# Cutting the first 4 MB load of a DMA-bound kernel into 16 and 112 partitions

## The chip, the cores and the metric

One core of a Trainium2 chip. Times are device microseconds (us) of that core. "Time" is the median of several executions; the profile is of one execution, and its span is about 1.4 us shorter than that execution's time (before: 119.5 against 120.87 us). A "row" is the 32 KB that a transfer moves into one SBUF partition; in the traces it is one packet on one of the 16 DMA engines (1536 packets of 32 KB, 96 to an engine). From the prediction on, "engine" without a name means a DMA engine, and its "ring" is what has been issued to it and is still to be moved.

## The reference

```python
# x, y: (1024, 16, 512) bf16; gamma: (512,) bf16
def reference(x, y, gamma):
    return x + gamma * y
```

x, y and the result are 16.78 MB each. The 16384 rows of 512 elements are laid over 128 SBUF partitions, 128 rows to a partition, and worked in four pieces of 32 rows: 32 KB per partition, 4 MB per transfer.

## The kernel before

```python
PIECES = [32, 32, 32, 32]
X_AT = [0, 32, 0, 32]            # two buffers for x
SP = [('x', 0), ('y', 0), ('x', 1), ('y', 1), ('y', 2), ('x', 2), ('y', 3), ('x', 3)]
ACT = [('g',), ('s', 0, 0, 2), ('s', 1, 1, 2), ('s', 2, 2, 2), ('s', 3, 3, 3)]
...
xv = xf.rearrange("(p n) d -> p n d", p=P)     # partition p: 128 rows, contiguous in HBM
...
elif kind == "x":                # loads are issued from SyncE, in the order of SP
    c = args[0]
    i = eng.dma_start(out=x_tile(c), in_=xv[:, piece(c), :]).then_inc(s_x[c], 16)
...
for c in range(n):               # VectorE
    yt = y_sb[:, piece(c), :]
    _take(s_y[c], 16, nc.vector)
    nc.vector.tensor_tensor(out=yt, in0=yt, in1=gamma_sb[...], op=MULT).then_inc(s_dve, 1)
    _take(s_x[c], 16, nc.vector)
    _take(s_dve, 1, nc.vector)
    nc.vector.tensor_tensor(out=yt, in0=x_tile(c), in1=yt, op=ADD).then_inc(s_add, 1)
```

The third x waits for the first add, the fourth for the second; the four stores are issued from ScalarE after the third and the fourth add. The first x, the first y and gamma are moved to the head of the program.

Of the kernel before, what the change touches and what calls it, by code (L numbers as in the profile page):

```python
# [3 lines left out]


PIECES = [32, 32, 32, 32]

X_AT = [0, 32, 0, 32]
X_AFTER = [-1, -1, 0, 1]


SP = [('x', 0), ('y', 0), ('x', 1), ('y', 1), ('y', 2), ('x', 2), ('y', 3), ('x', 3)]
ACT = [('g',), ('s', 0, 0, 2), ('s', 1, 1, 2), ('s', 2, 2, 2), ('s', 3, 3, 3)]

EARLY = [('x', 0), ('y', 0), ('g',)]
MULT, ADD = mybir.AluOpType.mult, mybir.AluOpType.add


def _take(sem, n, eng):


    return eng.wait_ge(sem, n).then_inc(sem, -n)  # L22


def kernel(
    tc: tile.TileContext,
    x: bass.AP,
    y: bass.AP,
    gamma: bass.AP,
    out: bass.AP,  # L30
):



    nc = tc.nc
    P = nc.NUM_PARTITIONS
    tc.close()
    tc.compile()  # L38

    xf = x.flatten_outer_dims()  # L40
    yf = y.flatten_outer_dims()
    of = out.flatten_outer_dims()
    N, D = xf.shape
    rows = N // P
    n = len(PIECES)
    assert sum(PIECES) == rows
    starts = [sum(PIECES[:c]) for c in range(n + 1)]
    dt = xf.dtype
    xv = xf.rearrange("(p n) d -> p n d", p=P)
    yv = yf.rearrange("(p n) d -> p n d", p=P)  # L50
    ov = of.rearrange("(p n) d -> p n d", p=P)

    gamma_row = nc.alloc_sbuf_tensor("gamma_row", [1, D], dt).ap()
    ones_row = nc.alloc_sbuf_tensor("ones_row", [1, P], dt).ap()
    gamma_sb = nc.alloc_sbuf_tensor("gamma_sb", [P, D], dt).ap()
    y_sb = nc.alloc_sbuf_tensor("y_sb", [P, rows, D], dt).ap()
    x_rows = max(a + r for a, r in zip(X_AT, PIECES))
    x_sb = nc.alloc_sbuf_tensor("x_sb", [P, x_rows, D], dt).ap()
    gamma_ps = nc.alloc_psum_tensor("gamma_ps", [P, D], mybir.dt.float32).ap()

    sem = nc.alloc_semaphore
    s_gamma, s_ones, s_ps, s_dve = sem("s_gamma"), sem("s_ones"), sem("s_ps"), sem("s_dve")
    s_x = [sem(f"s_x{c}") for c in range(n)]
    s_y = [sem(f"s_y{c}") for c in range(n)]
    s_add, s_end, s_out = sem("s_add"), sem("s_end"), sem("s_out")

    def piece(a, b=None):
        return slice(starts[a], starts[(a if b is None else b) + 1])

    def x_tile(c):  # L70
        return x_sb[:, X_AT[c] : X_AT[c] + PIECES[c], :]

    early, stores = [], 0

    def ring(eng, what, known=-1):

        nonlocal stores
        for w in what:
            kind, args = w[0], w[1:]
            need = X_AFTER[args[0]] if kind == "x" else args[2] if kind == "s" else -1  # L80
            if need > known:
                eng.wait_ge(s_add, need + 1)
                known = need
            if kind == "g":
                i = eng.dma_start(out=gamma_row, in_=gamma.unsqueeze(0)).then_inc(s_gamma, 16)
            elif kind == "x":
                c = args[0]
                i = eng.dma_start(out=x_tile(c), in_=xv[:, piece(c), :]).then_inc(s_x[c], 16)
            elif kind == "y":
                c = args[0]  # L90
                i = eng.dma_start(out=y_sb[:, piece(c), :], in_=yv[:, piece(c), :])
                i.then_inc(s_y[c], 16)
            else:
                r = piece(args[0], args[1])
                i = eng.dma_start(out=ov[:, r, :], in_=y_sb[:, r, :]).then_inc(s_out, 16)
                stores += 1
            if w in EARLY:
                early.append(i.ins)

    ring(nc.sync, SP)  # L100
    ring(nc.scalar, ACT)


    nc.vector.memset(ones_row, 1.0).then_inc(s_ones, 1)  # L104
    _take(s_ones, 1, nc.tensor)
    _take(s_gamma, 16, nc.tensor)
    nc.tensor.matmul(gamma_ps, ones_row, gamma_row, start=True, stop=True).then_inc(s_ps, 1)  # L107
    _take(s_ps, 1, nc.vector)
    nc.vector.tensor_copy(out=gamma_sb, in_=gamma_ps).then_inc(s_dve, 1)  # L109
    _take(s_dve, 1, nc.vector)  # L110

    for c in range(n):
        yt = y_sb[:, piece(c), :]
        _take(s_y[c], 16, nc.vector)
        nc.vector.tensor_tensor(  # L115
            out=yt, in0=yt, in1=gamma_sb[:, None, :].to_broadcast([P, PIECES[c], D]), op=MULT
        ).then_inc(s_dve, 1)
        _take(s_x[c], 16, nc.vector)
        _take(s_dve, 1, nc.vector)
        nc.vector.tensor_tensor(out=yt, in0=x_tile(c), in1=yt, op=ADD).then_inc(s_add, 1)  # L120


    nc.scalar.sem_inc(s_end, 1)
    _take(s_end, 1, nc.sync)
    _take(s_add, n, nc.sync)
    _take(s_out, 16 * stores, nc.sync)

    main = nc.main_func.blocks[0].instructions
    names = {i.name for i in early}
    for b in nc.main_func.blocks[1:]:  # L130
        for i in [i for i in b.instructions if i.name in names]:
            b.instructions.remove(i)
    for k, i in enumerate(early):
        main.insert(1 + k, i)


# [1 line left out]
_INS = ['x', 'y', 'gamma']  # L138
_OUTS = [((1024, 16, 512), 'bfloat16')]


# [23 lines left out]
```

## Time and profile before

| | before |
|---|---|
| time, median of 6 runs | 120.34 us (120.29 to 121.09) |
| span of the profiled run | 119.5 us |
| share of the 16 DMA engines | 98.9% |
| one 32 KB row on one DMA engine | 1.213 us |

The prediction below shows the lines that carry this. Three more are needed here, from the page (the busy share of the DMA engines and the GB/s, in 40 slices of the span), from the view of the x buffer (time from issue to landing), and from the view of a stretch (start:end and length, busy times of the engines, granted clock, DMA share, GB/s):

```profile
DMA  7989898998998989898989999898989898989995
GB/s 208 494 373 504 351 526 351 384 493 351 384 493 351 526 351 526 351 515 362 493 384 471 406 428 450 384 493 351 526 351 526 351 526 351 515 362 471 406 471 230
```

```profile
DMA to landing us min/median/max: 12.1/21.5/30.3
```

```profile
5.20:10.05 4.85, 0.21 (x1) 0.00 (x0) 0.69 (x1) 0.00 (x0) 1.00 1.00 432
```

Single slices swing between 350 and 526 GB/s because all engines start their 32 KB packets at nearly the same time (the first at 0.99 to 1.60 us) and a packet counts in the slice in which it starts. A stretch of exactly four rows (4 x 1.213 = 4.85 us) gives the true rate, 432 GB/s. The first x lands 12.1 us after its issue, the shortest of the four.

### The profile page before, as it was taken

The numbers are of one execution on the slowest core, as the hardware profiler recorded it, in microseconds if no ns is written. First come the engines' busy times: TensorE is split into PE (matmuls) and PEld (weight loads), VectorE is DVE, ScalarE is ACT, GpSimd is POOL, SyncE is SP. The second block draws the span as 40 slices with busy tenths as digits, with TensorE's granted clock in tenths as the row PEclk, the third lists the DMA queues.
The fourth block names the chain that finished last, engine by engine and source line by source line (L and its number), as shares of the span: only waits on it lengthen the run. The fifth ranks groups of instructions, "written<-read, shape, count | busy, mean of one in ns | idle before, by whom it ended". The sixth has DMA issues, their size and how long they took to land. (4 is left out here: it accounts for less than half of the span.)

```text
span 119.5 us, 84 instructions
## 1 busy us (share of the span) xinstructions
PE 0.6 (0%) x1; PEld 0.1 (0%) x1; DVE 70.2 (59%) x10; POOL 0.2 (0%) x4
## 2 busy tenths in 40 slices
PE   0100000000000000000000000000000000000000
PEld 0000000000000000000000000000000000000000
DVE  0100000699999289999999999999999600000000
POOL 0000000000000000000000000000000000000000
DMA  7989898998998989898989999898989898989995
GB/s 208 494 373 504 351 526 351 384 493 351 384 493 351 526 351 526 351 515 362 493 384 471 406 428 450 384 493 351 526 351 526 351 526 351 515 362 471 406 471 230
DMA packets 1730, 50.33 MB, mean 421 GB/s; under 512 B 193, under 2 KB 194, under 8 KB 194
## 3 DMA queue, kind: packets, MB, share of 16 engines
q1 hardware_dynamic: 1152, 33.55, 66.4%
q10 hardware_dynamic: 578, 16.78, 32.5%
HBM read 33.56 MB, written 16.78 MB: 421 GB/s over the span
## 5 line engine op out<-in xcount | busy, mean ns | idle before, releaser
L115 DVE TENSOR_TENSOR y_sb<-y_sb,gamma_sb 128x16384 bf16<-128x16384 bf16 x4 | 34.8, 8688 | 18.4 <-DVEq L22 18.4
L120 DVE TENSOR_TENSOR y_sb<-x_sb,y_sb 128x16384 bf16<-128x16384 bf16 x4 | 34.8, 8692 | 0.6
L109 DVE CAST gamma_sb<-gamma_ps 128x512 bf16<-128x512 f32 x1 | 0.7, 692 | 3.4 <-DVEq L22 3.4
L104 DVE MEMSET ones_row<- 1x128 bf16 x1 | 0.2, 165 | 2.0 <-PEq L38 2.0
L107 PE MATMUL gamma_ps<-gamma_row,ones_row 1*128 1x512 bf16 x1 | 0.6, 580 | 4.8 <-PEq L22 4.8
L107 PEld LDWEIGHTS gamma_ps<-gamma_row,ones_row 1*128 1x128 bf16 x1 | 0.1, 100 | 4.8 <-issue 4.8
L149 POOL MEMSET const-bfloat16-1.0<- 128x1 bf16 x1 | 0.1, 101 | 0.0
L149 POOL MEMSET const-uint8-127<- 128x1 uint8 x1 | 0.1, 101 | 0.0
L149 POOL MEMSET const-float32-0.0<- 128x1 f32 x1 | 0.1, 98 | 0.2 <-issue 0.2
L149 POOL MEMSET const-float32-1.0<- 128x1 f32 x1 | 0.1, 98 | 0.0
## 6 DMA issues: line engine op xcount, KB each, us to landing
x_sb<-in_x_dram SPq DMA_DIRECT2D x4, 4096.0 KB, 21.5
y_sb<-in_y_dram SPq DMA_DIRECT2D x4, 4096.0 KB, 35.4
out_dram<-y_sb ACTq DMA_DIRECT2D x4, 4096.0 KB, 23.8
gamma_row<-in_gamma_dram ACTq DMA_DIRECT2D x1, 1.0 KB
```

What stands on the lines that cost most here:

```text
L104: nc.vector.memset(ones_row, 1.0).then_inc(s_ones, 1)
L107: nc.tensor.matmul(gamma_ps, ones_row, gamma_row, start=True, stop=True).then_inc(s_ps, 1)
L109: nc.vector.tensor_copy(out=gamma_sb, in_=gamma_ps).then_inc(s_dve, 1)
L115: nc.vector.tensor_tensor(out=yt, in0=yt, in1=gamma_sb[:, None, :].to_broadcast([P, PIECES[c], D]), op=MULT).then_inc(s_dve, 1)
L120: nc.vector.tensor_tensor(out=yt, in0=x_tile(c), in1=yt, op=ADD).then_inc(s_add, 1)
L149: nc = _bacc.Bacc("TRN2", target_bir_lowering=False, num_devices=1)
```

## The change

The intent: the DMA engines stand idle for the first 0.99 us. If the head of the program asks for 16 partitions first, one row for each engine, the engines might get their first row sooner, while the other 112 partitions are still being issued. The core of the diff (the rest rewrites how the lists of transfers are kept, and moves nothing):

```diff
+FIRST = 16
...
             elif kind == "x":
-                c = args[0]
-                i = eng.dma_start(out=x_tile(c), in_=xv[:, piece(c), :]).then_inc(s_x[c], 16)
+                to = x_sb[:, w[3] : w[3] + w[2] - w[1], :]
+                r = slice(w[1], w[2])
+                if w == x_loads[0]:
+                    i = eng.dma_start(out=to[:FIRST], in_=xv[:FIRST, r, :])
+                    early.append(i.then_inc(s_load[w], 16).ins)
+                    i = eng.dma_start(out=to[FIRST:], in_=xv[FIRST:, r, :])
+                else:
+                    i = eng.dma_start(out=to, in_=xv[:, r, :])
+                i.then_inc(s_load[w], 16)
...
-        _take(s_x[c], 16, nc.vector)
+                _take(s_load[w], 32 if w == x_loads[0] else 16, nc.vector)
```

More of the change, by code (lines that the diff above doesn't have):

```diff
@@ L6 @@
 PIECES = [32, 32, 32, 32]
-X_AT = [0, 32, 0, 32]
-X_AFTER = [-1, -1, 0, 1]
-SP = [('x', 0), ('y', 0), ('x', 1), ('y', 1), ('y', 2), ('x', 2), ('y', 3), ('x', 3)]
-ACT = [('g',), ('s', 0, 0, 2), ('s', 1, 1, 2), ('s', 2, 2, 2), ('s', 3, 3, 3)]
-EARLY = [('x', 0), ('y', 0), ('g',)]
+SP = [('x', 0, 32, 0), ('y', 0, 32), ('x', 32, 64, 32), ('y', 32, 64), ('y', 64, 96), ('x', 64, 96, 0), ('y', 96, 128), ('x', 96, 128, 32)]
+ACT = [('g',), ('s', 0, 32, 2), ('s', 32, 64), ('s', 64, 96), ('s', 96, 128)]
+EARLY = (2, 1)
+DVE = [('m', 0), ('a', 0), ('m', 1), ('a', 1), ('m', 2), ('a', 2), ('m', 3), ('a', 3)]
+FIRST = 16
 MULT, ADD = mybir.AluOpType.mult, mybir.AluOpType.add
@@ L56 @@
     y_sb = nc.alloc_sbuf_tensor("y_sb", [P, rows, D], dt).ap()
-    x_rows = max(a + r for a, r in zip(X_AT, PIECES))
+    x_loads = [w for w in SP + ACT if w[0] == "x"]
+    y_loads = [w for w in SP + ACT if w[0] == "y"]
+    stores = [w for w in SP + ACT if w[0] == "s"]
+    for loads in (x_loads, y_loads, stores):
+        assert sum(w[2] - w[1] for w in loads) == rows
+    x_rows = max(w[3] + w[2] - w[1] for w in x_loads)
     x_sb = nc.alloc_sbuf_tensor("x_sb", [P, x_rows, D], dt).ap()
@@ L62, with meets, pieces_of, x_at @@
     s_gamma, s_ones, s_ps, s_dve = sem("s_gamma"), sem("s_ones"), sem("s_ps"), sem("s_dve")
-    s_x = [sem(f"s_x{c}") for c in range(n)]
-    s_y = [sem(f"s_y{c}") for c in range(n)]
-    s_add, s_end, s_out = sem("s_add"), sem("s_end"), sem("s_out")
-    def piece(a, b=None):
-        return slice(starts[a], starts[(a if b is None else b) + 1])
-    def x_tile(c):
-        return x_sb[:, X_AT[c] : X_AT[c] + PIECES[c], :]
-    early, stores = [], 0
-    def ring(eng, what, known=-1):
-        nonlocal stores
-        for w in what:
-            kind, args = w[0], w[1:]
-            need = X_AFTER[args[0]] if kind == "x" else args[2] if kind == "s" else -1
+    s_load = {w: sem("s_" + "_".join(map(str, w[:2]))) for w in x_loads + y_loads}
+    s_add, s_go, s_end, s_out = sem("s_add"), sem("s_go"), sem("s_end"), sem("s_out")
+    added = [a for kind, *a in DVE if kind == "a"]
+    order = {a[0]: k for k, a in enumerate(added)}
+    def meets(a, b, c, d):
+        return a < d and c < b
+    def pieces_of(a, b):
+        return [c for c in range(n) if meets(starts[c], starts[c + 1], a, b)]
+    def x_at(row):
+        return next(w[3] + row - w[1] for w in x_loads if w[1] <= row < w[2])
+    def frees(w):
+        old = x_loads[: x_loads.index(w)]
+        old = [v for v in old if meets(v[3], v[3] + v[2] - v[1], w[3], w[3] + w[2] - w[1])]
+        return [c for v in old for c in pieces_of(v[1], v[2])]
+    early = []
+    def ring(eng, what, n_early):
+        known, went = 0, False
+        for k, w in enumerate(what):
+            kind = w[0]
+            need = frees(w) if kind == "x" else pieces_of(w[1], w[2]) + list(w[3:]) if kind == "s" else []
+            need = max((order[c] + 1 for c in need), default=0)
+            if kind == "s" and not went and ("go",) in DVE:
+                _take(s_go, 1, eng)
+                went = True
             if need > known:
-                eng.wait_ge(s_add, need + 1)
+                eng.wait_ge(s_add, need)
                 known = need
@@ L86, in ring @@
             elif kind == "x":
-                c = args[0]
-                i = eng.dma_start(out=x_tile(c), in_=xv[:, piece(c), :]).then_inc(s_x[c], 16)
+                to = x_sb[:, w[3] : w[3] + w[2] - w[1], :]
[7 more added lines that the diff above has]
+                i.then_inc(s_load[w], 16)
             elif kind == "y":
-                c = args[0]
-                i = eng.dma_start(out=y_sb[:, piece(c), :], in_=yv[:, piece(c), :])
-                i.then_inc(s_y[c], 16)
+                r = slice(w[1], w[2])
+                i = eng.dma_start(out=y_sb[:, r, :], in_=yv[:, r, :]).then_inc(s_load[w], 16)
             else:
-                r = piece(args[0], args[1])
+                r = slice(w[1], w[2])
                 i = eng.dma_start(out=ov[:, r, :], in_=y_sb[:, r, :]).then_inc(s_out, 16)
-                stores += 1
-            if w in EARLY:
+            if k < n_early:
                 early.append(i.ins)
-    ring(nc.sync, SP)
-    ring(nc.scalar, ACT)
+    ring(nc.sync, SP, EARLY[0])
+    ring(nc.scalar, ACT, EARLY[1])
     nc.vector.memset(ones_row, 1.0).then_inc(s_ones, 1)
@@ L110, with need @@
     _take(s_dve, 1, nc.vector)
-    for c in range(n):
-        yt = y_sb[:, piece(c), :]
-        _take(s_y[c], 16, nc.vector)
-        nc.vector.tensor_tensor(
-            out=yt, in0=yt, in1=gamma_sb[:, None, :].to_broadcast([P, PIECES[c], D]), op=MULT
-        ).then_inc(s_dve, 1)
-        _take(s_x[c], 16, nc.vector)
-        _take(s_dve, 1, nc.vector)
-        nc.vector.tensor_tensor(out=yt, in0=x_tile(c), in1=yt, op=ADD).then_inc(s_add, 1)
+    landed, open_mults = set(), 0
+    def need(loads, c):
+        for w in loads:
+            if w not in landed and meets(starts[c], starts[c + 1], w[1], w[2]):
+                _take(s_load[w], 32 if w == x_loads[0] else 16, nc.vector)
+                landed.add(w)
+    for kind, *args in DVE:
+        if kind == "go":
+            if open_mults:
+                _take(s_dve, open_mults, nc.vector)
+                open_mults = 0
+            nc.vector.sem_inc(s_go, 1)
+            continue
+        c = args[0]
+        yt = y_sb[:, starts[c] : starts[c + 1], :]
+        if kind == "m":
+            need(y_loads, c)
+            g = gamma_sb[:, None, :].to_broadcast([P, PIECES[c], D])
+            nc.vector.tensor_tensor(out=yt, in0=yt, in1=g, op=MULT).then_inc(s_dve, 1)
+            open_mults += 1
+        else:
+            need(x_loads, c)
+            if open_mults:
+                _take(s_dve, open_mults, nc.vector)
+                open_mults = 0
+            at = x_at(starts[c])
+            xt = x_sb[:, at : at + PIECES[c], :]
+            nc.vector.tensor_tensor(out=yt, in0=xt, in1=yt, op=ADD).then_inc(s_add, 1)
     nc.scalar.sem_inc(s_end, 1)
@@ L125 @@
     _take(s_add, n, nc.sync)
-    _take(s_out, 16 * stores, nc.sync)
+    _take(s_out, 16 * len(stores), nc.sync)
     main = nc.main_func.blocks[0].instructions
```

## The prediction

> **What bounds the kernel now.** I read the page first for the shares, then the table of waits, then the timeline, then stretches of the span, and last the trace's records of single DMA packets, because the page alone does not say what one packet costs. The page of the kernel before:
>
> ```profile
> span 119.5 us, 84 instructions
> PE 0.6 (0%) x1; PEld 0.1 (0%) x1; DVE 70.2 (59%) x10; POOL 0.2 (0%) x4
> ...
> DMA packets 1730, 50.33 MB, mean 421 GB/s; under 512 B 193, under 2 KB 194, under 8 KB 194
> ...
> q1 hardware_dynamic: 1152, 33.55, 66.4%
> q10 hardware_dynamic: 578, 16.78, 32.5%
> ```
>
> VectorE is busy for 59% of the span, and the 16 DMA engines for 66.4 + 32.5 = 98.9% of it. So the DMA engines bound the kernel: only 1.1% of 119.5 us, 1.3 us, is idle on the average engine. The packet counts say what an engine gets. The load queue q1 has 1152 packets: eight transfers of 128 rows make 1024 data packets, and 8 x 16 = 128 are the small completion packets. A data packet is thus one whole partition row of 32 KB. The store queue has 4 x 128 + 4 x 16 = 576, and two more for gamma. Each engine moves (8 + 4) x 8 = 96 rows.
>
> The chain of waits that ended last does not help here: it names one add on VectorE (7%), and stops where DMA begins. The table of waits says what VectorE lacked:
>
> ```profile
> DVE y_sb L115 <- DVEq L22: 18.4, 2, 15.8
> ```
>
> The multiply of piece 0 waits 15.8 us and that of piece 1 another 2.6 us (18.4 less 15.8), both for y to land. The timeline gives the order:
>
> ```profile
> 0.00 0.37 SPq L88 DMA_DIRECT2D x_sb<-in_x_dram  x1
> 0.12 0.52 ACTq L85 DMA_DIRECT2D gamma_row<-in_gamma_dram  x1
> ...
> 0.42 0.42 SPq L91 DMA_DIRECT2D y_sb<-in_y_dram  x1
> ...
> 22.06 8.69 DVE L115 TENSOR_TENSOR y_sb<-y_sb,gamma_sb 128x16384 bf16<-128x16384 bf16 x1 [15.81 <-DVEq L22]
> ...
> 77.17 17.78 ACTq L95 DMA_DIRECT2D out_dram<-y_sb  x4
> ```
>
> The reader is to see that the first x is issued at 0, y 0.42 us later, and that the stores begin at 77.17 us. The stretches (the numbers before PEclk are engines' busy times; the last two are DMA share and GB/s) show where the DMA idles:
>
> ```profile
> 0.00:0.99 0.99, 0.00 (x0) 0.00 (x0) 0.00 (x0) 0.20 (x4) 1.00 0.00 0
> 0.99:3.30 2.31, 0.00 (x0) 0.00 (x0) 0.17 (x1) 0.00 (x0) 1.00 1.37 454
> 3.30:50.00 46.70, 0.58 (x1) 0.10 (x1) 25.91 (x4) 0.00 (x0) 1.00 1.00 423
> 50.00:80.00 30.00, 0.00 (x0) 0.00 (x0) 29.71 (x5) 0.00 (x0) 1.00 0.98 425
> 80.00:118.80 38.80, 0.00 (x0) 0.00 (x0) 14.43 (x2) 0.00 (x0) 1.00 1.00 432
> 118.80:119.60 0.80, 0.00 (x0) 0.00 (x0) 0.00 (x0) 0.00 (x0) 1.00 0.01 0
> ```
>
> Nothing moves in the first 0.99 us; from then to 118.8 us the share is about 1.00 (it exceeds 1 where a packet is counted wholly in the stretch in which it starts). The packet records agree: the first 32 KB packets start at 0.99 to 1.27 us on 15 engines and at 1.60 us on one, a packet takes 1.213 us in the median (32768 B / 1.213 us = 27.0 GB/s, times 16 = 432 GB/s), and the engines finish between 118.8 and 119.15 us. 96 x 1.213 = 116.4 us, plus 1.0 us of start, 0.4 us from the last packet to the span's end, and about 1.7 us of longer packets and gaps, is the span. The longest of those packets are the first ones: 15 take 1.82 to 2.14 us (the late starter 1.48), and all end at 2.8 to 3.2 us.
>
> [...]
>
> **The change part by part.** The rest of the diff is a rewriting; the order of instructions on each engine is the same in both, apart from one more transfer at SyncE's head. VectorE waits for 32 on the first x's semaphore, both halves together, so nothing on VectorE starts on a half.
>
> (a) *Start.* The aim is that the engines get their first row after a short issue. The first packet comes 0.99 us after the issue began, and the issue itself lasts 0.37 us. If a 16-row issue were shorter in proportion to rows (an estimate; issues of one row and of 128 rows took 0.52 and 0.33 to 0.48 us, so it may not be shorter at all), 0.3 us would be gained, and the late engine might lose its 0.5 us lag. The end is set by the last engine. I put this at -0.2 us, with -0.6 us the most.
>
> (b) *More work.* One more issue of about 0.4 us on SyncE, while every engine is busy with a row: hidden. Sixteen more completion packets, one per engine, of 9 ns in the records: +0.01 us.
>
> (c) *The 16 rows.* [...]
>
> (d) *The 112 rows.* [...]
>
> (e) *What follows.* From y on, all transfers have 128 partitions and the delay is only carried along. Nothing absorbs it: the engines have no idle time later, the multiply of piece 0 waits for y, which is behind x in the same rings, and the stores come from the same chain of VectorE. The third x, issued at 39.6 us, comes before the rings drain: five transfers of 8 x 1.213 = 9.7 us after 1 us of start last till 49.5 us, and they would last longer. So a delay of an engine goes to the end in full.
>
> Sum: -0.2 + 3.64 + (1.8 to 3.64) = +5.2 to +7.1 us, or 125.6 to 127.4 us.
>
> **The rivals.** *[...]the split is nearly free.* Then only (a) and (b) remain: 119.7 to 120.5 us, most likely 120.2. For it: [...]the change was meant to help.[...]
>
> *The 112 rows spread in strides.* If step j of all engines covers 16 neighbouring rows[...]: 8 x 3.64 = +29 us, near 149 us. It would be an odd layout to choose; I give it 5%.
>
> *VectorE becomes the bound*: its 70.2 us of work are unchanged and wait for y first; no.
>
> *Gamma comes late*: its packet shares an engine with the first rows; the matmul may move from 4.8 us to 8 us, still far ahead of 22 us. Hidden.
>
> **Range and chances.** [...]I predict 126.0 us, and a range of 119.7 to 130.0 us holds both. Faster by over 2% would need under 117.9 us; 1.0 us of idle start is all there is to take, so 1%. Within 2%: 33%. Slower: 66%.
>
> **What would show it.** The packet records of the changed kernel: if (c) is right, the first 16 packets take near 4.8 us and not 1.8 to 2.1; if (d) is right, some of the following packets take around 2.4 us, and the first x lands at 15 to 19 us instead of 12.1, the smallest time from issue to landing of an x in this kernel. The DMA share stays near 1.00, as a held packet counts as busy, but the GB/s of the first slices falls to about 100 and then rises. The first multiply would start at 26 to 30 us instead of 22.06. If the first packets last as before, [...]the time is at 120.2 us[...]. A start that moves from 0.99 us by over 0.3 us would make (a) wrong.

The marks are cuts: what no trace of this case shows is taken out. With it go all of (c) and (d), and a rival by which only some of the engines take the 16 rows, with a time of 120.2 to 120.5 us. In the sum 3.64 us (3 x 1.213) stands for the 16 rows of (c) and 1.8 to 3.64 us for the 112 rows of (d): both were my estimates, and nothing measured before the change showed them. With -0.2 us for (a) the sum came to +5.2 to +7.1 us. Two thirds of the chances went to a loss of some such kind, most of it at +3.5 to +9 us, one third to the two rivals near 120.2 us.

## The result, and the profile after

129.75 us in the median of 6 runs (129.43 to 130.38), against 120.34 us. The ratio is 1.0769, with a 95% interval of 1.073 to 1.0808: slower by 9.4 us. (A ratio is the mean time of one kernel's fast runs over the mean of the other's of the same rounds, so not quite the ratio of the medians.) The page of the kernel after:

```profile
span 128.1 us, 85 instructions
## 1 busy us (share of the span) xinstructions
PE 0.6 (0%) x1; PEld 0.1 (0%) x1; DVE 70.2 (55%) x10; POOL 0.2 (0%) x4
...
DMA  9879979998999999989989999999899899899894
GB/s 164 164 184 307 297 194 338 471 450 379 471 450 389 471 409 420 471 379 460 450 379 471 450 389 471 409 420 471 379 460 471 368 460 460 379 471 450 389 471 184
...
q1 hardware_dynamic: 1168, 33.56, 68.2%
```

VectorE's 70.2 us are the same. The DMA share is full as before, though the kernel is slower: a packet that is held up counts as busy (from 5 to 20 us the share is 0.98 at 251 GB/s). It is the GB/s that show it. The first seven slices (3.2 us each) are at 164 to 338, and from the eighth on the row looks as before. The 16 packets more than before (1168 against 1152) are the second set of completions.

Stretches of the same trace, then its DMA issues (count, KB, us from issue to landing), then its timeline:

```profile
1.00:5.00 4.00, 0.00 (x0) 0.00 (x0) 0.17 (x1) 0.00 (x0) 1.00 1.30 197
5.00:20.00 15.00, 0.58 (x1) 0.10 (x1) 0.69 (x1) 0.00 (x0) 1.00 0.98 251
...
32.00:50.00 18.00, 0.00 (x0) 0.00 (x0) 16.73 (x2) 0.00 (x0) 1.00 1.01 435
```

```profile
x_sb<-in_x_dram SPq DMA_DIRECT2D x1, 3584.0 KB, 21.1
x_sb<-in_x_dram SPq DMA_DIRECT2D x1, 512.0 KB, 6.9
```

```profile
31.35 8.69 DVE L159 TENSOR_TENSOR y_sb<-y_sb,gamma_sb 128x16384 bf16<-128x16384 bf16 x1 [23.18 <-DVEq L25]
...
85.78 17.78 ACTq L123 DMA_DIRECT2D out_dram<-y_sb  x4
```

The 16 rows land after 6.9 us. The 112 rows, issued at 0.43 us, land at 21.5 us, where the whole x landed at 12.1 us. The first multiply starts at 31.35 us instead of 22.06, and the stores at 85.78 instead of 77.17. The delay arises before 22 us and is then carried along.

The trace's records of single packets give it row by row. They don't name the engine: a packet is put down to the engine whose packet before it ends as this one starts (within 0.13 us in these two traces, most within 0.01). The table has means over the 16 engines, in us; row k is the (k+1)-th row of each engine.

| | row 0 ends | rows 1 to 7 take | row 8 (y) takes | last engine ends |
|---|---|---|---|---|
| before | 3.07 | 8.50 | 1.21 | 119.15 |
| after | 4.89 | 14.85 | 1.73 | 127.66 |
| difference | +1.82 | +6.35 | +0.52 | +8.5 |

The three differences make 8.7 us. The profiled run of before, a slow one of its kind (120.87 us), has rows of 1.23 to 1.33 us between 17 and 38 us, which the trace after does not have; that hides 0.7 us, and the engine that ends last is 0.5 us further behind the mean than before. 8.7 + 0.5 = 9.2, near the 9.4 us of the times.

The first packets start at 1.01 to 1.84 us, before at 0.99 to 1.60: nothing was gained at the start.

### The profile page after: what moved, and what is told of

Its sections match the earlier page's. It is cut to its first block, busy times and chain, and to the rows that moved or that the text cites. A ratio compares the mean times of both kernels' runs of the same rounds, so it can differ in the third digit from the quotient of the medians.

```text
span 128.1 us, 85 instructions
## 1 busy us (share of the span) xinstructions
PE 0.6 (0%) x1; PEld 0.1 (0%) x1; DVE 70.2 (55%) x10; POOL 0.2 (0%) x4
## 3 DMA queue, kind: packets, MB, share of 16 engines
q1 hardware_dynamic: 1168, 33.56, 68.2%
## 6 DMA issues: line engine op xcount, KB each, us to landing
x_sb<-in_x_dram SPq DMA_DIRECT2D x1, 3584.0 KB, 21.1
```

## The experiments

My theory was that the engines get in each other's way, by which partitions they write at the same time; the mechanism that I had in mind is shown by no run. The rivals: a second transfer at the head costs by itself; the rows chosen are slow to read from HBM; only one of the two halves hurts. In experiments 2 to 4, 7 and 11 to 14 extra loads go ahead of the kernel before's own. They go to parts of the buffers that are loaded over later, after a wait, so all results were right.

### Experiment 1: cut along the columns

```diff
-dma_start(out=to[:16], in_=xv[:16, r, :]);    dma_start(out=to[16:], in_=xv[16:, r, :])
+dma_start(out=to[:, :4, :], in_=xv[:, :4, :]); dma_start(out=to[:, 4:, :], in_=xv[:, 4:32, :])
```

> The first x goes as two transfers too, but cut along the columns: 128 partitions x 4 KB (the same 512 KB as the 16 rows), then 128 x 28 KB. My theory[...] the time is that of the kernel before, 120.3 us within 0.5. Rival (a second transfer at the head costs by itself, through its issue or its completion): 122 us or more. The gain the change hoped for: an earlier first packet than 0.99 us; I expect none.

120.79 us against 120.25 us, ratio 1.0039 (1.0016 to 1.0061). So two transfers at the head cost 0.5 us when each has all 128 partitions, not 9.4. (This kernel has the whole rewriting of the change, so that isn't the cause either.) The first packet started at 1.01 us, no sooner than before. Its issues, from the view of the DMA:

```profile
x_sb<-in_x_dram SPq DMA_DIRECT2D x1, 3584.0 KB, 11.6
x_sb<-in_x_dram SPq DMA_DIRECT2D x1, 512.0 KB, 3.6
```

The same 512 KB and 3584 KB land after 3.6 and 11.6 us instead of 6.9 and 21.1. How the bytes are cut matters, and not that they are cut.

### Experiments 2, 3 and 4: the 16 rows alone, and where they go

```diff
+dma_start(out=y_sb[:16,     96:128, :], in_=xv[:16,     r, :])   # 2: neighbouring partitions
+dma_start(out=y_sb[0:112:7, 96:128, :], in_=xv[:16,     r, :])   # 3: same rows, partitions 7 apart
+dma_start(out=y_sb[:16,     96:128, :], in_=xv[0:112:7, r, :])   # 4: other rows, neighbouring partitions
 dma_start(out=to, in_=xv[:, r, :])                               # the whole first x
```

> The kernel before with one more load ahead of the first x: rows 0 to 15 of x into partitions 0 to 15 of a part of y's buffer that is loaded over later (result stays right). It is the 16-row half of the change by itself, with the rest of x left whole. If the 16 rows cost what they cost in the changed kernel: first packets 3.7 us in the mean instead of 1.93, and 120.3 + 1.2 (one more row per engine) + 1.8 = 123.3 us. If the 16 rows are harmless and only the 112 hurt: first packets near 1.9 us, 121.6 us.

> As the 16-row load ahead of x, from the same 16 rows of HBM, but into partitions 0, 7, 14, ... 105[...].[...] twelve of the first packets near 1.9 us, four longer, 121.6 to 122.2 us. Rival (the rows' places in HBM are slow to read together): as with partitions 0 to 15, 3.7 us and 123.3 us.

> As the 16-row load ahead of x, into partitions 0 to 15 again, but from rows 0, 7, 14, ... 105 of HBM.[...] nothing changes against the load from rows 0 to 15: first packets 3.7 us, 123.3 us. HBM rival: first packets near 1.9 us, 121.6 us.

Single runs (state unknown): 124.45, 122.71 and 124.67 us, against 120.25 for before. Landing of the extra load in experiments 2, 3 and 4, in this order:

```profile
y_sb<-in_x_dram SPq DMA_DIRECT2D x1, 512.0 KB, 6.8
```

```profile
y_sb<-in_x_dram SPq DMA_DIRECT2D x1, 512.0 KB, 5.2
```

```profile
y_sb<-in_x_dram SPq DMA_DIRECT2D x1, 512.0 KB, 7.2
```

The first packets took 3.60, 1.91 and 3.67 us in the mean. Reading other rows changes nothing; writing to other partitions does. The HBM rival falls for these 16 rows. Experiment 2 prices the 16-row half: 124.45 - 120.25 - 1.21 for the row itself = 3.0 us (experiment 4: 3.2 us). Both are over the 123.3 us that I expected, since the row behind the 16 is held up too: it took 2.31 and 2.52 us in the mean. Experiment 3 came out 0.5 us above my limit of 122.2 us: its packets were fast, but the row behind them took 1.79 us. One of its packets took 2.77 us and the other 15 took 1.26 to 2.20, so the four longer ones that I expected don't stand out. Its first packet came 0.4 us later (1.38 us) than in experiments 2 and 4. Its first issue took longer too, 0.60 us instead of 0.38, and so it is in experiments 10 to 14: first issues of 0.56 to 0.60 us, first packets at 1.34 to 1.37 us. Why these issues take longer is not shown.

### Experiment 7: the 112 rows alone

```diff
+dma_start(out=y_sb[16:, 96:128, :], in_=xv[16:, r, :])
 dma_start(out=to, in_=xv[:, r, :])
```

> The kernel before with one more load ahead of the first x: rows 16 to 127 of x into partitions 16 to 127 of a part of y's buffer that is loaded over later. It is the 112-row half of the change by itself. Seven rows per engine would take 8.5 us without a loss. My prediction's count[...] gives 1.8 to 3.6 us of loss: 130.6 to 132.4 us. If the 112 rows cost what the changed kernel's trace shows (14.85 us for them and 0.5 us for the row behind): 120.3 + 8.5 + 6.8 = 135.6 us.

134.98 us against 120.31 us, ratio 1.1202 (1.1146 to 1.1257). The loss is 134.98 - 120.31 - 8.49 (seven rows of 1.213) = 6.2 us, well over the 1.8 to 3.6 us that I had counted. With the 3.0 us of the 16 rows that makes 9.2 us, about the change's whole loss of 9.4: the two halves add up (one of them from a single run), and the larger part is the 112 rows. The extra load lands after 17.2 us:

```profile
y_sb<-in_x_dram SPq DMA_DIRECT2D x1, 3584.0 KB, 17.2
```

### Experiments 8 and 9: which rows an engine gets

```diff
-dma_start(out=to[16:], in_=xv[16:, r, :])
+for j in 1..7: dma_start(out=to[16*j : 16*j+16],  in_=xv[16*j : 16*j+16, r, :])  # 8: strides
+for j in 0..6: dma_start(out=to[16+j : 128 : 7],  in_=xv[16+j : 128 : 7, r, :])  # 9: sevens
```

> The first x as eight transfers of 16 neighbouring partitions each, [...]the layout in strides, made by hand. If the one 112-row transfer is laid out in strides, this takes as long as the changed kernel, 129.7 us within 1. If it is laid out in neighbouring sevens, strides are worse: [...]3 us lost per row or a little less: 137 to 144 us.

> The first x as the 16 rows and then seven transfers of 16 partitions each, the j-th taking partitions 16 + j, 23 + j, ... 121 + j: [...]the layout in neighbouring sevens, made by hand. If the one 112-row transfer is laid out so, this takes as long as the changed kernel, 129.7 us, plus up to 0.5 for six more sets of completion packets. If the 112 rows are laid out otherwise: 125 to 127 us, the time that my prediction counted for sevens.

Experiment 9 took 129.61 us (ratio to before 1.0754), the changed kernel 129.75. Its seven rows took 2.85, 2.25, 1.72, 1.84, 1.99, 2.18 and 2.04 us in the mean, those of the 112-row transfer 2.82, 2.29, 1.66, 1.89, 2.01, 2.16 and 2.05. So the transfer of 112 partitions behaves as neighbouring sevens do, as I had assumed. Experiment 8 took 146.41 us (ratio 1.214), 2.4 us more than the most that I expected. In it all of x goes in transfers of 16 neighbouring partitions; here are four of its rows:

```profile
10.45:28.40 17.95, 0.00 (x0) 0.00 (x0) 0.00 (x0) 0.00 (x0) 1.00 1.01 117
```

Every row of x after the first takes 4.47 to 4.51 us, 3.7 times 1.213, at 117 GB/s instead of 432.

### Experiment 10: two halves

```diff
-FIRST = 16
+FIRST = 64
```

> The first x cut at partition 64 instead of 16: two transfers of 64 partitions[...].[...] 8 x 1.21 = 9.7 us lost, 130 us; [...]5 to 8 us lost, 125 to 128 us. Rival (only odd sizes like 16 and 112 are bad): 120.3 us.

130.66 us against 120.31 us, ratio 1.0833 (1.0785 to 1.0882): even worse than the change. Two rows of it:

```profile
4.45:9.50 5.05, 0.00 (x0) 0.00 (x0) 0.40 (x1) 0.00 (x0) 1.00 1.01 208
```

Rows take 2.55 us, 2.1 times 1.213, at 208 GB/s, about half of 432. The loss of 130.66 - 120.31 = 10.3 us is near the 9.7 us that I put first; the 5 to 8 us that I had read into the 16 rows ahead of this run were wrong. The rival that only odd sizes hurt falls.

### Experiments 11 to 14: four sets of 16 partitions

Why did the sevens lose 6.2 us, where I had counted 1.8 to 3.6? I sent the same set of 16 partitions four times in a row, so that the same partitions are written together in every row:

```diff
+spare = [x_sb[comb, 32:64, :]] + [y_sb[comb, 32*q : 32*q+32, :] for q in (1, 2, 3)]
+for to_spare in spare:
+    dma_start(out=to_spare, in_=xv[comb, r, :])
 dma_start(out=to, in_=xv[:, r, :])
# comb: 11:117:7 in 11, 3:109:7 in 12, 0:112:7 in 13, 28:92:4 in 14
```

> Four transfers of 16 partitions each ahead of the kernel before's loads, all to partitions 11, 18, 25, ... 116 (four different spare parts of the buffers, loaded over later)[...] rows take 1.21 us (the first one about 1.9 for its start-up) and the time is 120.3 + 4 x 1.21 = 125.2 us.[...]

> The same with partitions 3, 10, 17, ... 108[...]. Theory A[...]: 14 engines at 1.21 us per row, two at about 2.56, so the last engine is 4 x 1.35 = 5.4 us late: near 130 us. Theory B[...]: all 16 engines at well over 1.21 us in rows 1 to 3, in step.

> The same with partitions 0, 7, 14, ... 105[...]. Theory A: 12 engines at 1.21 us, four at 2.56, time as with one pair. Theory B: all engines slow, as with one pair or more so.

> Four 16-row transfers once more, to partitions 28, 32, 36, ... 88[...]. If it takes two pairs to hold up all engines: 14 engines at 1.2 to 1.5 us in rows 1 to 3 and two at about 2.4, as with the other single pair, near 131 us. If the place matters[...]: all 16 at about 2.49 us in rows 1 to 3, near 130.4 us.

A "pair", in the expectations and in the names of these runs, is two rows of a set that I expected to slow each other; why I expected it of these partitions is shown by no run. The records give neither the engine nor the partition of a packet. What is measured is how many of the 16 packets of a row are slow:

| experiment | partitions | slow rows forecast (theory A) | row 1 of the 16 engines (us) | time (us) | ratio to before |
|---|---|---|---|---|---|
| 11 | 11, 18, ... 116 | none | 1.22 to 1.24, all | 127.02 | 1.0533 |
| 12 | 3, 10, ... 108 | two | 1.22 to 1.36 on 14, 2.43 on two | 132.35 | 1.0976 |
| 14 | 28, 32, ... 88 | two | 1.22 to 1.38 on 14, 2.55 on two | 131.29 | 1.0893 |
| 13 | 0, 7, ... 105 | four | 2.45 to 2.50, all | 130.45 | 1.0827 |

Row 1 of experiment 11, and rows 1 to 3 of experiment 13, as stretches:

```profile
3.10:4.33 1.23, 0.00 (x0) 0.00 (x0) 0.00 (x0) 0.00 (x0) 1.00 1.01 426
```

```profile
3.20:10.67 7.47, 0.58 (x1) 0.10 (x1) 0.86 (x2) 0.00 (x0) 1.00 1.01 211
```

In experiment 11 the 16 partitions of row 1 run at 426 GB/s. So it is not the small number of partitions that hurts, but which of them are written together. Nor is it the reading: experiments 11 and 13 read rows of the same distance in HBM, seven partitions apart. In row 1 of experiments 12 and 14 only two of the 16 packets are slow, as theory A says. In experiment 13 all 16 engines take 2.49 us in each of rows 1 to 3, not only four, as theory B says. Experiment 14 came out as its first alternative said (near 131 us, two slow rows); but only one set held up all 16, and why it does is not shown.

Neither theory covers every row. In row 2 of experiment 12 five engines other than the two slow ones take 1.44 to 2.29 us; they begin by 5.1 us, while the first engine goes on to the rows of x at 7.00. In row 2 of experiment 11, where all of row 1 is fast, five take 1.41 to 1.64 us. And in experiment 3, which sends the set of experiment 13 for a single row, that row is not slow (its mean is 1.91 us, that of the first row of experiment 11 1.92, of experiment 13 2.28). So the table shows what happens when one set is written row after row in step; a rule for engines out of step does not come out of it.

Of the times of this group only that of experiment 14 was met; experiments 11 and 12 took 1.8 and 2.4 us more than expected, and 12 and 14 come out above 13. Once the first engines go on to the rows of x, slow rows follow (row 4 takes about 1.8 us in the mean in experiment 11, 2.3 in experiment 14), up to 4 us on single engines; I take it that they are held up by the late ones, which is argued. The late engines then cost a second time, which the trace of experiment 12 shows: y lands later, VectorE starts its first multiply at 34.01 us (experiment 13: 32.13), and the first store is issued at 88.45 us, when most engines have run out of loads:

```profile
86.00:89.30 3.30, 0.00 (x0) 0.00 (x0) 3.30 (x2) 0.00 (x0) 1.00 0.28 119
```

In the same stretch of experiment 13 the DMA share is 0.88. The rows before tell more than these times.

No version beat the kernel before, which stays the best of all that ran.

## Why the prediction was right, point by point

The direction held: slower, by the partitions that are written together. Why these hold each other up is not shown. The size was short: 126.0 as the point, and 5.2 to 7.1 us in the sum, where 9.4 us came. That 129.75 us still lies in the range of 119.7 to 130.0, by 0.25 us, is luck: the range was made to hold the rivals too, its upper end came from no sum, and 9.4 us lies over the +3.5 to +9 us that were to have most of the weight of a loss. The step that was mis-sized is (d).

- **What bounds the kernel, and (e), that nothing absorbs a delay:** right. The multiply moved by 9.3 us and the end by 8.6 us of the span. No wait took the delay up.
- **(a), a gain of 0.2 us at the start:** wrong. A first load of 16 rows of 32 KB (the change), of 128 rows of 4 KB (experiment 1) and of 128 rows of 32 KB (before) all started their first packet at 0.99 to 1.01 us. With 64 rows (experiment 10) it came later, at 1.34 us.
- **(b), the second issue and its completions hidden:** nearly right; experiment 1 has both and loses 0.5 us, with 144 packets more (1874 against 1730).
- **(c), +3.64 us for the 16 rows:** right in kind, 3.0 us in experiment 2. In the trace after, 16 packets are under way at a time, and the next one starts when one ends (within 0.13 us), so a row that is held up also holds up those behind it. I had estimated four times 1.213, 4.85 us, for the row; rows to 16 neighbouring partitions take 4.49 us in steady state (experiment 8). That is 0.36 of the 0.6 us; the rest may be the start-up of the first packet, which takes 0.7 us more than 1.213 in the kernel before. That is argued, not shown.
- **(d), +1.8 to 3.6 us for the 112 rows: the term that was mis-sized.** It was 6.2 us (experiment 7). The layout in neighbouring sevens was guessed rightly (experiment 9). The estimate was not: it charged a delay only to those rows that I took to slow each other, 1.8 us in the mean, or (8.5 + 1.8)/7 = 1.47 us per row. The trace after has a mean of 14.85/7 = 2.12 us, and none of the 112 packets passed at 1.213: the quickest took 1.44 us, in step 2. Steps 2 and 3 are the quickest in the mean, 1.66 and 1.89 us, while the others take 2.0 us and more. Experiment 13 shows all 16 engines at 2.49 us in three rows, where theory A had four of them slow. So rows are held up that I had not charged; by what rule stays open.
- **The rivals:** a split that is nearly free, and the rows on some of the engines only, are out by the 9.4 us and by 16 first packets that started within 0.83 us (1.01 to 1.84). The strides are out by experiments 8 and 9 (made by hand they took 146.41 us, where I had put them near 149). Late gamma was hidden, as said: the matmul started at 6.75 us.
- **What would show it:** the first 16 packets were to take near 4.8 us and took 3.7; the first x was to land at 15 to 19 us and landed at 21.5; the multiply at 26 to 30 us came at 31.35. All three have the sign of (c) and (d), and the last two the excess of (d). The DMA share stayed full as forecast, and the GB/s of the first slices fell to 164, not to about 100.

## What to carry to other kernels

If a load has to be cut, cut it along the free dimension, not along the partitions: the first cost 0.5 us here (experiment 1), while a transfer of 16, 64 or 112 neighbouring partitions cost about 3, 10 (both halves) and 6 us (experiments 2, 10 and 7). A full DMA share in a profile doesn't mean a full rate (0.98 at 251 GB/s here, against 432); look at the GB/s beside it. And when you expect some of the packets of a step to slow each other, don't charge only those: test whether the rest is held up too, as all 16 were in experiment 13 (2.45 to 2.50 us).
